# First batch's decay rates loaded by token pairs, row-half sums, two-step head dots and a new order of work in an RWKV attention and Fourier MLP kernel

## The chip, the cores and the metric

The kernel runs on one core of a Trainium2 chip. The core has five engines that run side by side: TensorE (PE, matrix products into eight PSUM banks), VectorE (DVE), ScalarE (ACT), GpSimd (POOL) and SyncE (SP, whose queue issues nearly all transfers). They wait for each other through semaphores. The metric is the device time of one execution in microseconds, the lower the better: a median of 181.98 us over three runs (181.62, 182.01 and 181.98).

## The reference

Inputs r, k, v and w have the shape (4 batches, 8 heads, 768 tokens, 48), in float32. For each batch and head a 48 x 48 state runs over the tokens:

```python
for t in range(S):
    cur = np.einsum('bhd,bhe->bhde', u[None] * kt, vt)
    y[:, :, t] = np.einsum('bhd,bhde->bhe', rt, state + cur)
    state = wt[:, :, :, None] * state + np.einsum('bhd,bhe->bhde', kt, vt)
...
X = np.fft.fft(np.fft.fft(x, axis=1), axis=2)     # x is y as (4, 768, 384)
u = x + np.real(X).astype(np.float32)
un = (u - mu) / np.sqrt(var + 1e-06)               # over the 384 columns
return u + np.maximum(un @ w_ch1, 0.0) @ w_ch2     # 384 -> 1536 -> 384
```

The output is (4, 768, 384) in float32.

## The kernel before

A batch's 768 tokens are cut into six chunks of 128 tokens, token on partition, and a pair such as (1, 4) below is batch 1, chunk 4. Attention of a chunk goes by these steps, with the names in the profile:

- four loads on SP's queue, each 192 KB in rows of 48 floats: `in_w`, `in_k`, `in_r`, `in_v` (line 622). Seven buffers of each kind stand for seven chunks.
- ACT takes the logarithm of w (`lb`, line 590). PE multiplies it with a mask (`msk`, line 795) for the sum over the earlier tokens. The sum that includes the token itself comes in one of several ways: `sum_two`, a second product with another mask (`nle`, line 818), or `sum_add`, an addition on DVE (line 832). Small products (lines 806 and 809) give each half head's total for the state's decay.
- ACT takes the exponentials (`e`, line 822; in the bank, line 848). DVE or POOL multiplies r and k with them (`rkh`, lines 849 and 576). PE transposes the two (lines 890 and 902) and ACT or DVE copies the result to `rkt` (lines 599 and 600); for the six chunks of batch 3 a transposing transfer on SP's queue does it instead (line 880).
- PE makes the 128 x 128 scores of each head (line 913, 48 rows at a time on two halves of the array), DVE masks them (`ah`, line 923), PE multiplies them and the state with v (lines 978 and 975) and brings the state forward (lines 950 and 947), and DVE applies the decay (line 958).
- The current token's term is r times k times u (`rk`, line 576, on POOL or DVE), summed over a head's 48 columns by one DVE reduction (`dc`, line 863), times v (`vtd`). It is added to the chunk's result in `x` (line 989 and others).

After a batch's six chunks the Fourier mix folds `x` (`sd`, `xf`), multiplies with cosine and sine tables (lines 1054 to 1059), copies (`hcs`, `hcr`), multiplies again (line 1098), and adds x (`uf`, lines 1115 and 1128). The mean is taken off (`un`), by batch statistics on DVE (`bst`, `agg`, lines 1155 and 1157) in batches 1 to 3, and in batch 0 by a sum that comes out of the addition itself, with the variance from a square on ACT. The normalised rows are transposed by PE and copied (`unt`), or transposed by a transfer (line 1180), in halves of three chunks. The MLP then takes for each half 36 products of 128 x 384 with the first matrix (line 1205), a clamp at zero on ACT or DVE (`ht`), and 36 with the second (line 1224), and DVE adds and scales (`osb`, line 1233) before the store.

What sets the order: each step is recorded as an operation, often with several ways and several engines to choose from, and a table of numbers, `ORDER`, written out per engine, picks the ways and the sequence. Each engine runs its list in that sequence and waits where a step needs another engine's. A planner's costs (`dur`, `xfer`, `T_LAT`) do not move the lists, they only decide which PSUM bank a step gets. PE's list has 32 filler products into a bank that nobody reads (line 1291).

## Time and profile before

| | us |
|---|---|
| median of three runs | 181.98 |
| profiled execution, time | 181.76 |
| profiled execution, span | 179.6 |
| PE busy | 172.1 |
| DVE busy | 159.5 |
| ACT busy | 127.5 |
| POOL busy | 107.7 |
| first MLP product of batch 0 starts (line 1205) | 41.4 |
| first MLP product of batch 1 starts (line 1205) | 84.5 |
| last MLP product ends | 177.1 |

The span runs from the first to the last instruction of the profiled execution; 2.16 us of its time lie around it. A group's row gives the line, engine, operation, output and inputs, count, then busy us in all and mean ns of one, then the engine's idle time just before them and what ended it. Products and DVE instructions overlap their neighbours a little, so the pitch from one to the next is shorter than a row's mean.

### The profile page before, as it was taken

Reading aid. Unit: us, or ns where it says so; the run is one execution under the profiler, and the core shown is the slowest. Engines: PE = TensorE matmul, PEld = TensorE weight load, DVE = VectorE, ACT = ScalarE, POOL = GpSimd, SP = SyncE. Lnnn points to the kernel's source line nnn. Section 1 sums busy time; section 2 is a strip of 40 time slices with the busy share of each in tenths; the row PEclk is TensorE's granted clock in tenths of the full one; section 3 lists DMA queues with packets and bytes.
Section 4 is the critical chain, followed back from the end, with each engine's and each line's share of the span. In section 5 each row is a group of like instructions: output and inputs, shape, how many; then the busy total and the mean of one; then the engine's idle time right before and its main releaser. Section 6 shows DMA issues by size and latency. Waiting matters only on the chain.

```text
span 179.6 us, 4554 instructions
## 1 busy us (share of the span) xinstructions
PE 172.1 (96%) x1704; PEld 113.7 (63%) x1704; DVE 159.5 (89%) x378; ACT 127.5 (71%) x306; POOL 107.7 (60%) x134
## 2 busy tenths in 40 slices
PE   4989899999999999999999999999989999999994
PEld 2456556766666667777666666766656766655663
DVE  7899899989999899999999999999999997971643
ACT  2899978679996578799999897989960775062200
POOL 2557969496705888499999964997862140500000
PEclk9999999999999999999999999999999999999999
DMA  6999999999999689999997999989972213034033
GB/s 118 217 210 225 183 206 193 203 216 179 162 205 204 145 173 224 199 211 217 202 239 137 224 182 240 235 155 197 245 71 56 74 47 65 1 60 141 0 131 131
DMA packets 117302, 29.28 MB, mean 163 GB/s; under 512 B 112545, under 2 KB 117282, under 8 KB 117282
## 3 DMA queue, kind: packets, MB, share of 16 engines
q1 hardware_dynamic: 115698, 26.65, 72.3%
q0 software_dynamic: 1584, 2.36, 7.9%
q8 instruction: 13, 0.21, 0.5%
q14 instruction: 7, 0.06, 0.1%
HBM read 23.59 MB, written 4.72 MB: 158 GB/s over the span
## 4 chain that ended last, share of the span: by engine, by line
PE 72%; DVE 13%; ACT 7%; POOL 3%; DMA 3%; issue 1%; POOLq 0%; DVEq 0%; ACTq 0%
PE bank L1205 23%; PE bank L1224 23%; PE bank L1098 4%; PE bank L1054 3%; PE bank L913 3%; DMA rkt<-rkh 3%; PE bank L890 2%; PE bank L795 2%; PE bank L978 2%; DVE bst L1155 2%; PE bank L975 1%; DVE uf L1128 1%; ACT rkt L599 1%; PE bank L950 1%; PE bank L818 1%
## 5 line engine op out<-in xcount | busy, mean ns | idle before, releaser
L1224 PE MATMUL bank<-w,ht 128*128 128x384 bf16 (+2 forms) x300 | 53.1, 320 | 0.0
L1205 PE MATMUL bank<-unt,w 128*128 128x384 bf16 x288 | 52.9, 326 | 0.0
L1213 ACT ACTIVATE ht<-bank 128x384 bf16<-128x384 f32 x70 | 31.0, 496 | 21.1 <-PE bank L1205 20.9
L1224 PEld LDWEIGHTS bank<-w,ht 128*128 128x128 bf16 x300 | 27.8, 98 | 15.6
L1205 PEld LDWEIGHTS bank<-unt,w 128*128 128x128 bf16 x288 | 26.6, 98 | 15.8 <-ACT ht L1213 0.2
L923 DVE TENSOR_TENSOR ah<-bank,msk 128x512 bf16<-128x512 f32 x44 | 28.7, 682 | 0.8 <-PE bank L913 0.6
L576 POOL TENSOR_TENSOR rk<-in_r,in_k 128x384 f32<-128x384 f32 x22 | 21.8, 999 | 1.9 <-issue 1.4
L576 POOL TENSOR_TENSOR rkh<-in_k,e 128x384 bf16<-128x384 f32 x18 | 18.0, 1003 | 6.7 <-ACT e L836 4.9
L576 POOL TENSOR_TENSOR rk<-rk,ub 128x384 f32<-128x384 f32 x20 | 19.8, 998 | 3.3 <-DVE rk L576 2.1
L576 POOL TENSOR_TENSOR vtd<-in_v,dc 128x384 f32<-128x384 f32 x20 | 16.4, 829 | 5.1 <-DVE sd L576 1.8
L599 ACT ACTIVATE rkt<-bank 128x512 bf16<-128x512 bf16 (+1 forms) x23 | 16.3, 713 | 4.3 <-PE bank L902 2.8
L1233 DVE SCALAR_TENSOR_TENSOR osb<-bank,rstd,uf 128x384 f32<-128x384 f32 (+2 forms) x24 | 14.3, 594 | 5.5 <-PE bank L1224 3.5
L1211 DVE TENSOR_SCALAR ht<-bank 128x384 bf16<-128x384 f32 x26 | 13.5, 548 | 5.4 <-PE bank L1205 5.2
L863 DVE TENSOR_REDUCE dc<-rk 128x8 f32<-128x384 f32 x24 | 12.7, 544 | 0.4 <-POOL rk L576 0.4
L848 ACT ACTIVATE bank<-bank 128x384 f32<-128x384 f32 x22 | 10.6, 488 | 3.0 <-PE bank L795 2.7
L590 ACT ACTIVATE lb<-in_w 128x384 bf16<-128x384 f32 x24 | 12.6, 528 | 0.1
L590 ACT ACTIVATE un<-uf,agg 128x384 bf16<-128x384 f32 x19 | 11.2, 618 | 1.5 <-DVE agg L1157 0.9
L849 DVE TENSOR_TENSOR rkh<-bank,in_r 128x384 bf16<-128x384 f32 x22 | 11.9, 547 | 0.2 <-ACT bank L848 0.2
L590 ACT ACTIVATE vb<-in_v 128x384 bf16<-128x384 f32 x22 | 11.5, 530 | 0.4 <-DMA in_v<-in_v_dram 0.3
L822 ACT ACTIVATE e<-bank 128x392 f32<-128x392 f32 (+1 forms) x18 | 8.8, 498 | 3.9 <-PE bank L809 2.5
L978 PE MATMUL bank<-vb,ah 128*128 128x48 bf16 x192 | 11.2, 183 | 0.0
L576 POOL TENSOR_TENSOR xf<-sd 128x384 bf16<-128x384 f32 (+1 forms) x7 | 6.9, 1002 | 6.1 <-DVE xf L576 3.9
(178 smaller groups left out, 365.1 us busy)
## 6 DMA issues: line engine op xcount, KB each, us to landing
in_r<-in_r_dram SPq DMA_DIRECT2D x24, 192.0 KB, 3.9
in_k<-in_k_dram SPq DMA_DIRECT2D x24, 192.0 KB, 3.8
in_w<-in_w_dram SPq DMA_DIRECT2D x24, 192.0 KB, 3.8
in_v<-in_v_dram SPq DMA_DIRECT2D x24, 192.0 KB, 3.8
out_dram<-osb SPq DMA_DIRECT2D x23, 192.0 KB, 2.9
w<-in_moe_w_ch_dram POOLq DMA_DIRECT2D x2, 576.0 KB, 7.9
w<-in_moe_w_ch_dram POOLq DMA_DIRECT2D x1, 1152.0 KB, 10.7
out_dram<-osb SPq DMA_DIRECT2D x1, 128.0 KB, 1.8
```

Source lines behind the costliest of these rows:

```text
L576: return lambda e: e.tensor_tensor(out=o, in0=a, in1=b, op=f)
L590: return lambda e: e.activation(o, a, f, **kw)
L599: {"act": lambda e: e.activation(o(), i(), ACTF.Copy), "dve": lambda e: e.tensor_copy(out=o(), in_=i())}, **kw)
L849: op("dve", v_1(DM), lambda e: e.tensor_tensor(out=rh[:, :, 0:D], in0=ps(tce)[:, 0:DM].rearrange("t (h d) -> t h d", d=D), in1=rt[:, :, :] ...
L863: op("dve", v_1(DM), lambda e: e.tensor_reduce(out=dc[:, :], in_=rku[:, :, :], axis=mybir.AxisListType.X, op=ALU.add), r=[("RK", i2)], w=[ ...
L923: masked[n].append(op("dve", v_1(512), lambda e: e.tensor_tensor(out=ah[:, x:H:2, :], in0=ps(bk)[:, :].rearrange("p (h t) -> p h t", t=128 ...
L978: ins = e.matmul(ps(ty)[:, D * h:D * h + D], ah[:, h, :], vb[:, h, :], start=first and not ype, stop=True, skip_group_check=True)
L1205: ins = e.matmul(ps(t)[:, 0:384], W1[:, m, 256 * (j // 2) + j % 2:256 * (j // 2) + 256:2], unt[:, :, m, :], start=(m == 0), stop=(m == NM ...
L1211: {"dve": lambda e, j=j, t=t, ht=ht: e.tensor_scalar(out=ht[:, j, :], in0=ps(t)[:, 0:384], scalar1=su, scalar2=0.0, op0=ALU.mult, op1=ALU. ...
L1213: "act": lambda e, j=j, t=t, ht=ht: e.activation(ht[:, j, :], ps(t)[:, 0:384], ACTF.Relu, scale=su)},
L1224: ins = e.matmul(ps(t)[:, 0:hi - lo], ht[:, j, 128 * x:128 * x + 128], W2[:, j, lo:hi], start=(j == 0), stop=(j == NJ - 1))
L1233: op("dve", v_1(hi - lo) + 64, lambda e: e.scalar_tensor_tensor(out=o[:, lo:hi], in0=ps(t)[:, 0:hi - lo], scalar=rstd[:, kb:kb + 1], in1=u ...
```

## The change

For batch 0 alone (`PAIRED = 1`) the six loads of w become three, each of 256 tokens: token 2p lies beside token 2p + 1 on partition p, so that a row is 96 floats. The sums over tokens are then made for a pair of chunks at once: two logarithms (even and odd tokens), and for each of the two sums four products that each use half of the array's rows, with four new 128 x 128 masks (`PM`, which DVE makes in a buffer that `unt` uses later), and 16 (for the last pair 8) small products for the totals. The exponential of the totals becomes two narrow ACT instructions in place of a wider single one. All 'sum' ways of batch 0 fall away.

The reduction over a head's 48 columns may be made in two steps, adding two halves of 24 and then reducing 24 columns (`dots`). Three chunks use it: (0, 1), (0, 3) and (1, 0). Four half-batch columns of `uf`, three in batch 2 and one in batch 3, use a new way (`add_sum`): the sum comes out of the addition, and ACT's square gives the variance, in place of the batch statistics. Some planner costs change (load 985 to 998, `T_LAT`, a shift by 200), and the table `ORDER` is new on all five engines.

Beside the pairs, the table picks other ways for some chunks: chunks (1, 4), (1, 5) and (2, 1) take `sum_add` in place of `sum_two` while (1, 0) goes the other way; chunk (1, 4) is transposed by a transfer and no longer by PE.

SP's queue at the start of the program; the digit behind a name is the buffer, here the chunk of batch 0, and in the changed kernel `in_w` is one tensor with all buffers. Before:

```order
L622 DMA in_r1<-in_r_dram 128x8x48
L622 DMA in_k1<-in_k_dram 128x8x48
L622 DMA in_w1<-in_w_dram 128x8x48
L622 DMA in_w0<-in_w_dram 128x8x48
L615 DMA osb0<-in_u_dram 1x384
L622 DMA in_r0<-in_r_dram 128x8x48
L622 DMA in_k0<-in_k_dram 128x8x48
L622 DMA in_w2<-in_w_dram 128x8x48
L622 DMA in_v0<-in_v_dram 128x8x48
```

Now:

```order
L634 DMA in_r1<-in_r_dram 128x8x48
L634 DMA in_r0<-in_r_dram 128x8x48
L634 DMA in_k1<-in_k_dram 128x8x48
L643 DMA in_w<-in_w_dram 128x8x96
L623 DMA osb0<-in_u_dram 1x384
L634 DMA in_k0<-in_k_dram 128x8x48
L634 DMA in_k2<-in_k_dram 128x8x48
L643 DMA in_w<-in_w_dram 128x8x96
L634 DMA in_v0<-in_v_dram 128x8x48
```

The loads of w for two chunks have become one, and those of r and k stand closer to the front.

PE just after the first fillers; `lb` is the logarithm of w, `msk` and `nle` are the old masks, `unt0` holds the new ones. Before:

```order
L656 MATMUL bank1<-osb0,vtd3 128x384
L795 MATMUL bank2<-lb0,msk 128x384
L818 MATMUL bank3<-lb0,nle 128x384
L795 MATMUL bank4<-lb1,msk 128x384
L749 MATMUL bank5<-ss,unt1 128x193
```

Now:

```order
L687 MATMUL bank1<-osb0,vtd3 128x384
L839 MATMUL bank2<-lb0,unt0 128x384
L839 MATMUL bank3<-lb0,unt0 128x384
L839 MATMUL bank2<-lb1,unt0 128x384
L839 MATMUL bank3<-lb1,unt0 128x384
L839 MATMUL bank4<-lb0,unt0 128x384
L839 MATMUL bank5<-lb0,unt0 128x384
```

Each sum of a chunk has become two half-row products into the same bank, and the products of both chunks alternate.

DVE in batch 0's first chunks, from the first product of r with its exponential (`rkh`) on; `rk` is r times k, `dc` the head sums, `vtd` the current token's term. Before:

```order
L863 TENSOR_REDUCE dc1<-rk1 128x8
L849 TENSOR_TENSOR rkh1<-bank4,in_r1 128x8x48
L849 TENSOR_TENSOR rkh0<-bank2,in_r0 128x8x48
L863 TENSOR_REDUCE dc0<-rk0 128x8
L576 TENSOR_TENSOR rkh1<-in_k1,e2_1 128x8x48
L587 MEMSET rkh2 128x8x8
L600 COPY rkt0<-bank4 128x512
L576 TENSOR_TENSOR vtd0<-in_v0,dc0 128x384
```

Now:

```order
L608 COPY ub<-bank1 128x384
L922 TENSOR_TENSOR rkh0<-bank2,in_r0 128x8x48
L922 TENSOR_TENSOR rkh1<-bank3,in_r1 128x8x48
L595 MEMSET rkh0 128x8x8
L584 TENSOR_TENSOR rk0<-rk0,ub 128x384
L584 TENSOR_TENSOR rkh0<-in_k0,e2_0 128x8x48
L584 TENSOR_TENSOR rk1<-rk1 128x8x24
L940 TENSOR_REDUCE dc0<-rk0 128x8
L940 TENSOR_REDUCE dc1<-rk1 128x8
```

The head sums have moved behind both products with r, one of them has an addition of halves (`rk1<-rk1`) ahead of it, and the copy of `ub` has come to DVE from ACT.

The diff, without the table:

```diff
-PSUM_STATE, NE = 1, 16
+PSUM_STATE, NE, PAIRED = 1, 16, 1
...
+INW = sb("in_w", [NIN, H, D], FP32)
+INB["w"] = [INW[:, i, :, :] for i in range(NIN)]
+PM = UNT[0].rearrange("p a b t -> p (a b t)")[:, 0:512].rearrange("p (x t) -> p x t", x=4)
...
+    def load_pair(b, c):
+        i = (b * NC + c) % NIN
+        loads[b, c, "w"] = loads[b, c + 1, "w"] = op("sp", 750, lambda e: e.dma_start(
+            INW[:, i:i + 2, :, :].rearrange("p a h d -> p (a h d)").rearrange("p (h x) -> p h x", h=H),
+            w[b, :, c * CH:(c + 2) * CH, :].rearrange("h (p a) d -> p h (a d)", a=2)),
+            w=[("in", "w", i), ("in", "w", i + 1)], sem="in_w%d" % i, xfer=1400)
...
+        for x, (f0, f1, s1) in enumerate(((ALU.subtract, ALU.is_gt, 0.0), (ALU.subtract, ALU.is_gt, 1.0),
+                                          (ALU.is_ge, ALU.mult, -1.0), (ALU.is_gt, ALU.mult, -1.0))):
+            dset(128, ts(PM[:, x, :], CI[:, 128:256], QP[:, :], s1, f0, f1), r=["CI", "QP", ("UNT", 0, 1)],
+                 w=["PM%d" % x] + ([("UNT", 0, 0)] if x == 0 else []))
...
+                    def cum(e, m=m):
+                        for x in range(2):
+                            for y in range(2):
+                                z = slice(64 * y, 64 * y + 64)
+                                ins = e.matmul(ps(sums[n + y, m])[:, 0:DM], PM[z, 2 * m + x, :], LB[l2[x]][z, :, 0:D],
+                                               start=x == 0, stop=x == 1, skip_group_check=True)
+                        for h in range(HP if m else 0):
+                            for x in range(2):
+                                for y in range(2 if c < NC - 2 else 1):
+                                    z = slice(64 * y, 64 * y + 64)
+                                    ins = e.matmul(ps(sums[n + y, m])[:, DM + 2 * h:DM + 2 * h + 2],
+                                                   LB[l2[x]][z, 2 * h:2 * h + 2, :].rearrange("t h d -> t (h d)"), ONE[z, :],
+                                                   start=x == 0, stop=x == 1, skip_group_check=True)
...
+        def dots(m):
+            if m < D:
+                vec(H * m, tt(rku[:, :, 0:m], rku[:, :, 0:m], rku[:, :, m:D], ALU.add), w=[("RK", i2)])
+            op("dve", v_1(H * m), lambda e: e.tensor_reduce(out=dc[:, :], in_=rku[:, :, 0:m],
+                                                            axis=mybir.AxisListType.X, op=ALU.add),
+               r=[("RK", i2)], w=[("DC", i2)])
+        g.choose(("dots", b, c), lambda: dots(D), lambda: dots(D // 2))
...
+                def add_sum(kb=kb, t=t):
+                    whole()
+                    op("dve", v_1(DM) + 60, lambda e: e.scalar_tensor_tensor(
+                        out=uf[:, kb, :], in0=ps(t)[:, 0:DM], scalar=1.0, in1=xb[:, kb, 0:DM], op0=ALU.mult, op1=ALU.add,
+                        accum_out=ms[:, kb, 2:3]), r=[t, ("X", i, kb)], w=[("UF", i, kb), ("SUM", i, kb)])
+                    normed(ms[:, kb, 0:1], ("MS", i, kb))
+                    op("act", a_sb(DM) + 190, act(xf[:, kb, 63:447], uf[:, kb, :], ACTF.Square, scale=-float(DM) ** -0.5,
+                                                  bias=ms[:, kb, 1:2], accum_out=agg[:, kb, 1:2]),
+                       r=[("UF", i, kb), ("MS", i, kb)], w=[("AGG", i, kb)] + [(z, i, kb) for z in ("XFe", "XFo", "XFn")])
+                g.choose(("u", b, kb), add_bank, add_row, add_parts, add_sum)
```

More of the change, by code (lines that the diff above doesn't have):

```diff
@@ L814, in total, with sum_pair @@
                 op("pe", mm(1, 5), tot, r=["ONE", "IDB", "PB0", "PB", ("LB", i2)], w=[t])
+        def sum_pair():
+            op("act", a_ps(DM), lambda e: e.activation(E2[i2][:, 0:DM], ps(tci)[:, 0:DM], ACTF.Exp), r=[tci], w=[("E2", i2)])
+            if not last:
+                for x in range(2):
+                    op("act", a_ps(4) + 20, lambda e, x=x: e.activation(
+                        E2[i2][64 * x:64 * x + 64, DM + x:DM + H:2], ps(tci)[64 * x:64 * x + 64, DM + x:DM + H:2], ACTF.Exp),
+                       r=[tci], w=[("E2", i2)])
         def sum_two():
@@ L844, in sum_key @@
             decays([("E2", i2)])
-        g.choose(("sum", b, c), sum_two, sum_add, sum_key)
+        if paired:
+            sum_pair()
+        else:
+            g.choose(("sum", b, c), sum_two, sum_add, sum_key)
         def rh_bank():
```

86 lines of the change are left out of this document (62 added, 24 removed), and 139 rows, old and new, of the table ORDER.

## The prediction

> **What bounds the kernel now.** I first cut the span at the two places where a batch's MLP begins, and read each engine's busy time and the idle clock there.
>
> ```profile
> core 0: us, PE busy (x) PEld busy (x) DVE busy (x) ACT busy (x) POOL busy (x), PEclk, DMA share, GB/s
> 0.00:9.00 9.00, 6.51 (x26) 2.97 (x26) 7.32 (x37) 5.27 (x7) 3.52 (x14) 1.00 0.85 168
> 9.00:41.40 32.40, 30.45 (x381) 20.57 (x381) 30.28 (x72) 27.65 (x63) 25.29 (x33) 1.00 1.07 205
> 41.40:84.50 43.10, 43.08 (x471) 29.64 (x469) 41.74 (x92) 35.52 (x87) 29.47 (x34) 1.00 0.99 192
> 84.50:134.50 50.00, 49.49 (x521) 32.60 (x518) 48.59 (x106) 44.78 (x113) 42.41 (x47) 1.00 0.97 193
> 134.50:179.60 45.10, 42.54 (x315) 27.87 (x312) 31.55 (x74) 14.25 (x39) 7.06 (x11) 1.00 0.25 71
> ```
>
> From 41.4 on PE never stops (43.08 of 43.10, then 49.49 of 50.00); before that its busy time holds fillers. The same windows for the filler line alone:
>
> ```profile
> 0.00:9.00 9.00, 0.98 (x5) 0.49 (x5) 1.00 0.85 168
> 9.00:41.40 32.40, 5.05 (x19) 1.63 (x19) 1.00 1.07 205
> 41.40:84.50 43.10, 2.60 (x8) 0.78 (x8) 1.00 0.99 192
> ```
>
> So up to 41.4 PE has slack, some of it filled, and DVE is the tight engine: idle 1.68 + 2.12 = 3.80 us there, then 1.36, then 1.41. Eight fillers still stand between 41.4 and 84.5, most of them late, when batch 0's MLP is used up and DVE finishes batch 1's mix. After 84.5 there is no filler, and the chain of waits is PE's to the end:
>
> ```profile
> 40.82 0.62 PE bank L913 x16
> 41.43 2.54 PE bank L1205 x15
> 48.45 0.33 PE bank L913 x8
> 57.85 1.95 PE bank L1224 x12
> 84.00 0.60 PE bank L913 x16
> 84.61 2.06 PE bank L1205 x12
> 89.31 0.45 PE bank L902 x8
> 128.63 4.57 DMA rkt<-rkh
> 133.24 0.40 PE bank L913 x8
> 170.51 6.54 PE bank L1224 x52
> 177.15 0.35 DVE osb L1233
> ```
>
> The pitch of a 384-column product is 1.95/12 = 0.1625 us. Hence the time is: the start of batch 0's first L1205 (41.43), plus PE's work to batch 1's first L1205 (84.5), plus PE's work to 177.1, with one stop in it, at 133.24.
>
> **The change part by part.**
>
> *After 84.5.* Counted from the two programs, PE's products from batch 1's first L1205 to the end are the same set in both. `add_sum`, three of whose four columns replace batch statistics in batch 2, lies here, relieves DVE and lengthens nothing on PE: 0. What can move is PE's one stop:
>
> ```profile
> 133.24 0.40 PE L913 MATMUL bank<-rkt 48*128 48x128 bf16 x8 [0.51 <-DMA rkt<-rkh]
> ```
>
> The last two transposing transfers follow each other there. In the new order of SP's queue other transfers stand between those of (3, 4) and (3, 5), and the scores come earlier on PE. Bounds: 0.51 and the drain around it gone (-0.7), nothing (0), another such stop (+0.5). I take -0.35, midway between the first two, since the shift of both sides is ordered, not timed.
>
> *Between the two first L1205.* Three `nle` products go (to `sum_add`): 3 x 0.1625 = -0.49. (1, 4) goes from PE to a transfer: 8 products, by
>
> ```profile
> 38.09 0.22 PE bank L890 x4
> ```
>
> 8 x 0.055 = -0.44. Two fillers fewer, 2 x 0.1625 = -0.33, which counts if they only filled. PE's bound on this stretch falls by 1.26. The transfer adds one to SP's queue, among the stores of batch 0 and loads of batch 2; if it lands late, PE's scores for (1, 4) wait, and MLP products stand beside them as cover. I put 0 on it.
>
> *Up to batch 0's first L1205*, on DVE. The groups of that window:
>
> ```profile
> L863 DVE TENSOR_REDUCE dc<-rk 128x8 f32<-128x384 f32 x6 | 3.3, 546 | 0.4 <-POOL rk L576 0.4
> L1115 DVE SCALAR_TENSOR_TENSOR uf<-bank,x 128x384 f32<-128x384 f32 x5 | 2.6, 555 | 0.4 <-PE bank L1098 0.4
> L600 DVE CAST hcs<-bank 128x386 bf16<-128x386 f32 x3 | 1.7, 597 | 0.4 <-PE bank L1057 0.4
> L989 DVE TENSOR_TENSOR x<-bank,vtd 128x384 f32<-128x384 f32 x3 | 1.6, 549 | 0.1
> L576 DVE TENSOR_TENSOR xf<-x 128x191 bf16<-128x191 f32 (+1 forms) x5 | 1.5, 349 | 0.0
> L600 DVE COPY rkt<-bank 128x512 bf16<-128x512 bf16 x3 | 1.2, 420 | 0.0
> L576 DVE TENSOR_TENSOR rk<-in_r,in_k 128x384 f32<-128x384 f32 x2 | 1.1, 548 | 0.0
> L832 DVE TENSOR_TENSOR e<-bank,lb 128x384 f32<-128x384 f32 x1 | 0.5, 547 | 0.0
> L581 DVE TENSOR_SCALAR cp<-cp 128x1 f32<-128x1 f32 x1 | 0.1, 141 | 0.0
> L581 DVE TENSOR_SCALAR nle<-osb 128x128 bf16<-128x128 f32 x1 | 0.2, 207 | 0.0
> ```
>
> Against DVE's list up to its last `unt` copy ahead of that product, the new list has: `rk` products six for three, 3 x 0.548 = +1.65; additions to `x` five for three, +1.10; the copy of `ub`, taken as an addition from a bank, +0.55; one more `uf`, +0.56; the new masks, 4 x 0.207 + 2 x 0.141 = +1.11. It loses two `hcs`, -1.20, one `e`, -0.55, and small pieces (a part of the sine tables, copies of `rkt`, a score mask), -0.72. Six reductions become four and two halves with one addition of halves on DVE (the other is POOL's), each of the three at the 0.349 of a 191-wide addition: 4 x 0.546 + 3 x 0.349 = 3.23 against 3.28, that is -0.05, which fills make up. So two steps cost as much as one. Sum +2.45 us of durations. Rows of one engine overlap:
>
> ```profile
> 9.12 0.56 DVE L576 TENSOR_TENSOR rk<-rk,ub 128x384 f32<-128x384 f32 x1
> 9.60 0.55 DVE L576 TENSOR_TENSOR rk<-in_r,in_k 128x384 f32<-128x384 f32 x1
> ```
>
> The second starts 0.48 after the first, which lasts 0.56, a ratio of 0.86: +2.1 us of time.
>
> This can go into DVE's 3.80 us idle. Two of its pieces:
>
> ```profile
> 0.81 0.06 DVE L587 MEMSET bhpi<- 128x1 f32 x1 [0.81 <-PEq L1310]
> 8.97 0.06 DVE L587 MEMSET cs<- 128x3 bf16 x1 [0.53 <-POOL cs L580]
> ```
>
> The first 0.81 stays. The waits for `hcs` and `uf` above (0.4 each) and one for the last copies (0.3) are the mix's latency and stay too. Some 1.9 can be filled; as rows waiting on loads and POOL rarely fit whole, I take 1.2 filled. Batch 0's first L1205 then starts 0.9 later (bounds: 2.1 later with nothing filled; 0.8 earlier, if all can be filled and the waits for `hcs` and `uf` go too and the loads come sooner).
>
> From there to the end of batch 1's mix DVE is repaid: fewer table pieces and copies of `unt`, folds on POOL. Its list up to batch 1's first `uf` is only 0.14 us of rows longer than before, which less the 1.2 filled gives -1.1. POOL gets 5.9 us of rows more and ACT 1.7 in the whole program; between 41.4 and 84.5 alone ACT has 43.10 - 35.52 = 7.6 idle and POOL 13.6, so I put 0 on both. If that cover fails it is POOL's, whose pieces DVE's reductions already wait for (0.4 on line 863's row).
>
> *Loads.* The 18 loads of r, k and v for batch 0 stand, six loads of w become three. One takes
>
> ```profile
> in_w<-in_w_dram SPq DMA_DIRECT2D x24, 192.0 KB, 3.8
> ```
>
> 3.8 us to land, but at 205 GB/s of the window the queue passes one in 196608 / 205 GB/s = 0.96. Rows twice as long move at least as many bytes per time: the window with 192-byte rows gives 205 / 1.07 = 192 GB/s at full share, the one with stores in 1536-byte rows 71 / 0.25 = 284. A pair thus costs between 1.92 (no gain) and 1.30 (the store's rate); I take 1.55, near the short rows: -0.37 each, -1.1 in all, bounds 0 and -1.9. [...] Either way the loads end at 30, when DVE, not a load, sets the pace: 0 in the sum. The price is at the front: ACT's two logarithms of a pair both wait for one load of 1.55 instead of the first for one of 0.96, 0.6 later by the queue; behind them on ACT stand the exponentials that DVE's `rkh` needs. r and k now come ahead of it on the queue, so DVE has `rk` to do meanwhile; this is part of why I fill 1.2 and not 1.9.
>
> *Sums by half rows*, PE: 24 products for 12. Eight 48-row products on two halves take 0.33 (48.45) against 0.45 for eight full ones (89.31), a ratio of 0.73, though with 128 columns: 24 x 0.1625 x 0.73 = 2.85 against 12 x 0.1625 = 1.95, +0.9. [...]
>
> **Sum.** At batch 1's first L1205 the later of two sides counts: PE +0.9 - 0.93 - 0.33 = -0.36, DVE -1.1. So -0.36, then -0.35 late: -0.7. The profiled execution's 181.76 (span 179.6 and 2.16 around it) becomes 181.05; its time lies 0.2 below the median 181.98, from which -0.7 gives 181.2.
>
> **Rivals.**
> - *DVE's idle is not filled* (slower). With nothing filled batch 0's first L1205 comes 2.1 later, at 43.5; PE's side is +2.1 - 1.26 = +0.84 and DVE's +0.14, and the late stop stays: 182.8. Its place is the front, where four masks and the larger load of w stand ahead of the first chunk's sums. For it: POOL, at 999 ns a piece, gets more of what DVE waits for:
>
> ```profile
> L576 POOL TENSOR_TENSOR rk<-in_r,in_k 128x384 f32<-128x384 f32 x22 | 21.8, 999 | 1.9 <-issue 1.4
> ```
>
> Against: the new list has work that needs only r and k at just that place. It decides if that product starts after 41.43 + 0.93 + 0.33 = 42.7, where PE's side turns from gain to loss. Chance 0.26.
> - *DVE is freed sooner* (faster): with the pairs early, all 1.9 and more filled, the first L1205 at 40.6; PE -0.8 - 1.26 = -2.1, DVE -1.8; with -0.35: 179.8. Against it stand the +2.45. Chance 0.12.
> - *No change*: PE's two sides cancel (first L1205 1.3 later) and the late stop stays: 181.6 to 182.3. Chance 0.15.
> - *New stops after 84.5*: there is no filler there, so an operand that is late costs its whole wait. Three like the 0.51 of 133.24, with the drain at the price 0.7 taken above, less the -0.36: +1.7 and about 183.5 at most; 0.09. For it: POOL has more rows, and SP's queue one transfer more between its loads.
>
> **Numbers.** My forecast 0.38, own range 180.6 to 181.6. 0.2% (0.36 us) is about what a measurement here can tell. Faster: 0.38 + 0.12 = 0.50; within: 0.15; slower: 0.26 + 0.09 = 0.35. The range 179.6 to 183.6 reaches from just below the faster rival to the end of the last one; what it leaves out is their bounds being passed, less than 2 in 10.
>
> **What would show it.** Right: batch 0's first L1205 at 42.0 to 42.6, batch 1's at about 84.1, PE's stretch from there to its end at about 92.2 (now 177.05 - 84.5 = 92.55), six fillers between them, and DVE idle up to the first at 2.6. Wrong: a first L1205 after 42.7; more than six fillers' worth of idle on PE ahead of batch 1's; waits for `rkt`, `ht` or `ah` on PE after it; or a reduction of 24 columns that takes 0.55 as the one of 48 does, which turns the two steps into +1.0 on DVE.

## The result: slower, 184.76 us

| | before | changed |
|---|---|---|
| median, us | 181.99 (181.62 to 182.01, 4 runs) | 184.76 (183.95 to 185.22, 4 runs) |
| profiled execution: time, span, us | 181.76, 179.6 | 184.74, 182.9 |
| batch 0's first MLP product (now line 1304), us | 41.38 | 45.17 |
| batch 1's first MLP product | 84.54 | 86.78 |
| from there to PE's end | 92.50 | 93.65 |

The ratio is 1.0152, with a 95% interval of 1.0115 to 1.019. The forecast was 181.2. Executions more than 1.5% longer than the fastest of their kernel are left out of the medians and ratios here and below.

The windows of the changed kernel, cut at the same places as those of before, with the first stretch cut finer:

```profile
core 0: us, PE busy (x) PEld busy (x) DVE busy (x) ACT busy (x) POOL busy (x), PEclk, DMA share, GB/s
0.00:9.00 9.00, 6.12 (x21) 2.89 (x21) 7.12 (x42) 4.98 (x6) 3.76 (x14) 1.00 0.84 183
9.00:14.00 5.00, 4.04 (x48) 2.26 (x46) 3.39 (x9) 3.37 (x11) 1.79 (x4) 1.00 1.18 235
14.00:18.00 4.00, 3.49 (x31) 2.27 (x32) 3.21 (x7) 3.07 (x5) 3.31 (x5) 0.67 1.10 238
18.00:22.00 4.00, 3.80 (x68) 2.50 (x65) 3.62 (x9) 3.52 (x10) 1.98 (x3) 0.90 0.95 182
22.00:45.20 23.20, 21.98 (x276) 14.85 (x274) 21.91 (x54) 19.73 (x43) 16.96 (x23) 1.00 1.06 202
45.20:86.80 41.60, 41.60 (x459) 28.36 (x458) 40.44 (x88) 37.06 (x95) 31.42 (x36) 1.00 0.89 174
86.80:136.80 50.00, 48.78 (x511) 32.20 (x510) 48.75 (x107) 41.98 (x108) 43.66 (x49) 1.00 0.99 198
136.80:182.90 46.10, 43.53 (x323) 28.29 (x321) 30.54 (x74) 16.13 (x44) 10.17 (x14) 1.00 0.25 70
```

Three things stand out. The stretch between the two first MLP products is shorter (41.6 us for 43.1) and full. Ahead of it, between 9 and 18, DVE is busy only 6.60 of 9 us, where it was busy 8.80 before, and the granted clock (the share of full speed that TensorE is allowed) falls to 0.67 and then 0.90, where it was 1.00 in every window of before. After 86.8 PE is idle 1.22 of 50 us, where it was idle 0.51. So the milestones give the loss as a sum: +3.79 up to the first product, -1.55 between the two, +1.15 after: +3.39 on PE's end, against the -0.7 that was forecast.

DVE up to batch 0's first MLP product, of before:

```profile
0.00:41.38 41.38, 36.94 (x406) 23.53 (x407) 37.59 (x108) 32.90 (x69) 28.78 (x45) 1.00 1.03 197
```

and of the changed kernel:

```profile
0.00:45.17 45.17, 39.40 (x433) 24.76 (x434) 39.23 (x119) 34.64 (x74) 27.76 (x46) 0.96 1.02 203
```

DVE's work grew by 39.23 - 37.59 = 1.64. Its idle time, of which the forecast fills 1.2, grew from 3.79 to 5.94, by 2.15. Between 9 and 18 alone it is idler by 2.2, as much as the whole growth. Its waits there, in the changed kernel (us in all, times, longest):

```profile
DVE ub L608 <- PE bank L687: 1.8, 1, 1.8
DVE xf L595 <- PEq L1409: 0.8, 1, 0.8
DVE ah L1001 <- PE bank L991: 0.8, 1, 0.8
DVE rkh L922 <- ACT bank L921: 0.6, 2, 0.4
DVE rkh L584 <- ACT e L882: 0.4, 1, 0.4
```

The largest is new: the copy of `ub`, which the change brought to DVE, waits 1.8 us for a product of PE. PE's own start, in order of time (start, us, operation, and in brackets the idle time before it and who ended it):

```profile
2.88 5.30 PE L1356 MATMUL bank<-w 128*128 128x384 bf16 x16 [2.88 <-DVE w L595]
7.97 1.25 PE L1390 MATMUL bank<-idw,msk 128*128 128x384 bf16 x5
9.15 0.91 PE L687 MATMUL bank<-osb,vtd 1*128 1x384 f32 x2
9.99 0.82 PE L839 MATMUL bank<-lb,unt 64*128 64x384 bf16 x8
...
11.73 0.40 PE L980 MATMUL bank<-idw,rkh 128*128 128x128 bf16 x4 [0.29 <-DVE rkh L922]
...
13.29 0.40 PE L980 MATMUL bank<-idw,rkh 128*128 128x128 bf16 x4 [0.67 <-DVE rkh L584]
...
15.31 0.61 PE L991 MATMUL bank<-rkt 48*128 48x128 bf16 x8 [0.51 <-ACT rkt L607]
...
17.14 1.46 PE L839 MATMUL bank<-lb,unt 64*128 64x384 bf16 x8
```

The first 16 products, the warm-up, run on `w`, which DVE fills with ones for the purpose. One of them lasts 514 ns at the median before and 528 now, a filler of the same shape behind them 326 and 327. They began at 2.27 before and begin at 2.88 now, took 4.22 in all and take 5.30, and the product for `ub` and the first sums stand behind them. Then come three short stops, and after them the eight half-row sums that took 0.82 us at 9.99 take 1.46 at 17.14 (1.10 where the clock does not fall, as a later profile shows).

After 86.8 the chain of waits no longer is PE's alone. It comes to PE at 124.66 from DVE:

```profile
117.92 1.04 DVE uf L1251 x4
118.96 0.86 DVE ms L1254
119.82 0.47 DVE uf L1251 x2
120.30 0.33 DVE ms L1254 x2
...
124.00 0.61 DVE ah L1001
```

Line 1254 is the small product in `add_sum` that turns the sum of a row into the mean and the bias of the square.

### The profile page after: what moved, and what is told of

The parts are those of the page before. It is cut to its first block, busy times and chain, and to the rows that moved or that the text cites. A ratio compares the mean times of both kernels' runs of the same rounds, so it can differ in the third digit from the quotient of the medians.

```text
span 182.9 us, 4618 instructions
## 1 busy us (share of the span) xinstructions
PE 173.3 (95%) x1719; PEld 113.6 (62%) x1719; DVE 159.0 (87%) x385; ACT 129.9 (71%) x318; POOL 113.0 (62%) x142
## 4 chain that ended last, share of the span: by engine, by line
PE 60%; POOL 15%; DVE 11%; ACT 4%; issue 3%; SPq 2%; DMA 2%; DVEq 0%
PE bank L1304 19%; PE bank L1323 18%; POOL rk L584 7%; POOL rkh L584 4%; PE bank L1356 3%; PE bank L1176 2%; POOL vtd L584 2%; DVE ah L1001 2%; DMA in_r<-in_r_dram 2%; SPq L634 2%; PE bank L991 2%; PE bank L1390 2%; POOL sd L584 2%; DVE osb L1332 1%; PE bank L1056 1%
## 5 line engine op out<-in xcount | busy, mean ns | idle before, releaser
L1312 ACT ACTIVATE ht<-bank 128x384 bf16<-128x384 f32 x73 | 33.2, 502 | 21.3 <-PE bank L1304 21.0
L1304 PEld LDWEIGHTS bank<-unt,w 128*128 128x128 bf16 x288 | 26.6, 98 | 15.5 <-DVE unt L608 0.2
L584 POOL TENSOR_TENSOR rk<-in_r,in_k 128x384 f32<-128x384 f32 x19 | 18.9, 1003 | 1.3 <-DVE rkh L584 0.5
L584 POOL TENSOR_TENSOR rkh<-in_k,e 128x384 bf16<-128x384 f32 x17 | 17.0, 1005 | 3.5 <-DVE rk L584 1.8
L1310 DVE TENSOR_SCALAR ht<-bank 128x384 bf16<-128x384 f32 x23 | 12.3, 550 | 6.7 <-PE bank L1304 6.6
L607 ACT ACTIVATE rkt<-bank 128x512 bf16<-128x512 bf16 (+1 forms) x19 | 14.9, 784 | 2.5 <-PE bank L980 1.8
L584 POOL TENSOR_TENSOR sd<-x 128x385 f32<-128x385 f32 x11 | 11.0, 1010 | 2.7 <-DVE xf L584 1.7
L940 DVE TENSOR_REDUCE dc<-rk 128x8 f32<-128x384 f32 (+1 forms) x24 | 12.2, 517 | 0.3 <-POOL rk L584 0.2
L1067 DVE TENSOR_TENSOR x<-bank,vtd 128x384 f32<-128x384 f32 x21 | 11.4, 548 | 1.1 <-PE bank L1056 1.0
L584 POOL TENSOR_TENSOR xf<-sd 128x382 bf16<-128x382 f32 (+1 forms) x9 | 8.9, 1002 | 5.1 <-DVE xf L584 4.9
L598 ACT ACTIVATE un<-uf,agg 128x384 bf16<-128x384 f32 x18 | 10.5, 621 | 1.8 <-DVE agg L1213 1.7
```

The costliest lines, as they stand in the source:

```text
L584: return lambda e: e.tensor_tensor(out=o, in0=a, in1=b, op=f)
L598: return lambda e: e.activation(o, a, f, **kw)
L607: {"act": lambda e: e.activation(o(), i(), ACTF.Copy), "dve": lambda e: e.tensor_copy(out=o(), in_=i())}, **kw)
L940: op("dve", v_1(H * m), lambda e: e.tensor_reduce(out=dc[:, :], in_=rku[:, :, 0:m], axis=mybir.AxisListType.X, op=ALU.add), r=[("RK", i2)] ...
L1304: ins = e.matmul(ps(t)[:, 0:384], W1[:, m, 256 * (j // 2) + j % 2:256 * (j // 2) + 256:2], unt[:, :, m, :], start=(m == 0), stop=(m == NM ...
L1310: {"dve": lambda e, j=j, t=t, ht=ht: e.tensor_scalar(out=ht[:, j, :], in0=ps(t)[:, 0:384], scalar1=su, scalar2=0.0, op0=ALU.mult, op1=ALU. ...
```

## The experiments

**The fill of `w` in its old place, and the other way round.** Two theories for the late start: the fill of `w`, moved from the fifth place on DVE's list to the ninth, delays the warm-up and all behind it; or DVE's new work does it alone, and the fill's place is hidden. Three kernels. In the changed kernel the fill goes first:

```diff
 DVE's list, from its start
+L595 MEMSET w 128x384
 L595 MEMSET xf 128x6x32
 L595 MEMSET lb 128x8x8
 ...
 L595 MEMSET rkh 128x8x8
-L595 MEMSET w 128x384
 L589 TENSOR_SCALAR unt<-tc 128x1
```

> The changed kernel with one DVE instruction moved: the fill of w with ones, which PE's 16 warm-up products wait for, is first on DVE's list (it started at 2.44 us). Theory A (the late fill and the colder warm-up that follows hold up PE's front, then ub and the first sums, and this goes through to the end): the warm-up starts at about 1.3 and ends near 6.5 instead of 8.0, DVE's wait for ub of 1.81 shrinks below 0.7, the first L1304 comes at about 44 instead of 45.2, and the time falls by 1.0 to 1.6 us against the changed kernel's 184.76. Rival B (the front has slack, and DVE's and ACT's order in chunks (0, 1) to (0, 3) sets batch 0's end): the first sums come earlier, but the first L1304 moves by less than 0.3 and the time by less than 0.4.

In the kernel before the fill goes behind three more instructions (the expectation counts four):

```diff
-L587 MEMSET w 128x384
 L587 MEMSET vtd 1x128
 L587 MEMSET lb 128x256
-L581 TENSOR_SCALAR ht<-osb,tn 128x194 x2
+L581 TENSOR_SCALAR ht<-osb,tn 128x194
+L587 MEMSET w 128x384
+L581 TENSOR_SCALAR ht<-osb,tn 128x194
```

> The kernel before with one DVE instruction moved: the fill of w with ones stands behind four other instructions, so that it starts at about 2.45 instead of 1.83 us, as in the changed kernel. Theory A (that fill is on the path): first L1205 0.6 to 1.5 us later than 41.4 and the time up by 0.6 to 1.5 against 181.98. Rival B: the front has slack, less than 0.3 in both.

And in the kernel before it goes to the head of the list:

> The kernel before with one DVE instruction moved: the fill of w is DVE's first instead of fifth, so that PE's warm-up starts at about 1.3 instead of 2.27 us. Theory A (PE's front is on the path in the kernel before as well): the first L1205 0.5 to 1.0 us earlier than 41.4 and the time as much lower than 182.0. Rival B (there the first sums wait for ACT's logarithms at 8.35, not for PE): the first L1205 moves by less than 0.2; and PE then stands idle between its warm-up and the first sums, so that the clock can fall and cost 0.3 to 1.0.

Measured: with the fill first, the changed kernel takes 183.86 (ratio to before 1.012, 1.0061 to 1.0179), its first MLP product starts at 44.20 and PE ends at 179.37, 0.97 and 1.06 sooner. In this pair of profiles what is won at the front arrives at the end. The times alone do not show it, since the intervals of the two ratios overlap. The kernel before with a late fill takes a median of 183.24 (1.0107, 1.004 to 1.0174); its first MLP products start at 42.15 and 85.31, both 0.77 later. In the profile PE's end is only 0.1 later, since the stop for `rkt` near 133 vanished from that execution. The kernel before with the fill first gains nothing (182.91, a ratio of 0.9999, 0.9956 to 1.0041): its first sums wait for ACT's logarithms, and its first MLP product starts at 41.26, 0.12 sooner.

**The changed kernel a second time.** It was run again beside the later experiments.

> The changed kernel itself, unedited, beside the three runs below on the same chip: both theories expect the 1.0152 (1.0115 to 1.019) of the first measurement, that is +2.7 us, a first L1304 at 44.6 to 45.2, a granted clock near 0.6 in some 3 us between 14 and 20 us, and one stop of about 1.1 us on PE near 123.

The median is 184.15 (182.45 to 184.93), beside 183.0 for before on that chip, where both scatter more; the ratio is 1.0061 (1.0017 to 1.0104), still slower, though by less than the 1.0152 of the first chip. Its profiled execution differs from the first where it tells most:

```profile
2.88 4.53 PE L1356 MATMUL bank<-w 128*128 128x384 bf16 x16 [2.88 <-DVE w L595]
7.24 0.98 PE L1390 MATMUL bank<-idw,msk 128*128 128x384 bf16 x5
8.15 0.91 PE L687 MATMUL bank<-osb,vtd 1*128 1x384 f32 x2
8.99 0.82 PE L839 MATMUL bank<-lb,unt 64*128 64x384 bf16 x8
```

With the fill at the same 2.88, the same 16 products take 4.53 and not 5.30, the sums start a whole microsecond sooner, the clock does not fall, and the first MLP product starts at 43.67 instead of 45.17. So 1.5 of the 3.79 is not in every execution. The two runs below that change nothing ahead of batch 1's MLP (the two small products, and the batch statistics) give this front twice more, 44.65 and 45.19, both with a fall of the clock. In all four it comes 2.3 to 3.8 later than before.

The 1.5 does not reach the end. This execution took 185.46, longer than most: PE stops 1.1 for `xf` ahead of batch 1's first product, then 0.56, 0.29 and 0.42 behind it, and ends at 181.13, later than the 180.43 of the first profile.

The same rows with the fill first:

```profile
1.31 4.35 PE L1356 MATMUL bank<-w 128*128 128x384 bf16 x16 [1.31 <-DVE w L595]
5.49 0.98 PE L1390 MATMUL bank<-idw,msk 128*128 128x384 bf16 x5
...
9.05 0.83 PE L839 MATMUL bank<-lb,unt 64*128 64x384 bf16 x8 [1.34 <-DVE ub L608]
```

The paired kernels profiled with the fill first all start these sums at 9.05 or 9.06, while their warm-up lasts from 4.19 to 5.30. With the late fill the start follows the warm-up: 4.53 gives 8.99, 4.97 gives 9.43, 5.30 gives 9.99 (10.10 in the run with batch statistics). So the fill's old place was cover for a warm-up of uncertain length. Moving it behind costs nothing with a short warm-up and about 1 us with a long one. The first theory holds with that condition.

**Fillers at PE's stops.** Is the fall of the clock a cost of its own, or does it only show that PE has nothing to do? The fill goes first, and eight fillers more stand ahead of the three stops:

```diff
-NW = 32
+NW = 40
 PE's list, chunk (0, 0)
+L1390 MATMUL bank<-idw,msk 128x384 x2
 L980 MATMUL bank<-idw,rkh 128x128 x4
 ...
 L780 MATMUL bank<-ss,idw 128x191 x2
+L1390 MATMUL bank<-idw,msk 128x384 x3
 L980 MATMUL bank<-idw,rkh 128x128 x4
 ...
+L1390 MATMUL bank<-idw,msk 128x384 x3
 L991 MATMUL bank<-rkt 128x128 x8
```

> The changed kernel with the fill of w first, as in the run that moved it, and eight more filler products on PE (0.1625 us each), one, three or two to four at each place where PE then stood idle for chunk (0, 0): ahead of the transposes of r, of k, and of the first scores. Theory A (PE's idle time between 10.5 and 15.3 us lets the granted clock fall to 0.5, and PE's chain of chunks (0, 0) to (0, 2) is then slow and on the path): the clock in 14 to 18 us reads 1.00 instead of 0.60, the first L1304 comes 0.6 to 1.2 us earlier than the 44.2 without these fillers, and the time falls by as much against 183.86. Rival B (the slow clock falls where PE waits anyway): the clock reads 1.00, but the first L1304 and the time move by less than 0.3.

The window from 14 to 18 with the fill first alone:

```profile
14.00:18.00 4.00, 3.59 (x52) 2.31 (x52) 3.14 (x7) 2.74 (x6) 3.31 (x4) 0.60 0.94 213
```

and with the fillers too, above it the stretch up to the first MLP product:

```profile
0.00:43.32 43.32, 39.23 (x441) 24.45 (x442) 38.69 (x119) 34.54 (x74) 27.87 (x46) 1.00 0.98 192
...
14.00:18.00 4.00, 3.39 (x63) 2.03 (x61) 3.43 (x8) 3.55 (x9) 3.46 (x5) 1.00 1.09 242
```

The clock stays at 1.00 and the first MLP product starts at 43.32, 0.88 sooner than with the fill first alone: more work on PE made the rest earlier. Is it the clock, or do the fillers help in another way? One product further on tells, with the fill first alone (first row), with the fillers too (second), and in the second profile of the changed kernel, which has neither the fillers nor the fall (third):

```profile
19.16 0.88 PE L1076 MATMUL bank<-vtd,ht 128*128 128x384 f32 x2
```

```profile
18.25 0.88 PE L1076 MATMUL bank<-vtd,ht 128*128 128x384 f32 x2
```

```profile
18.18 0.88 PE L1076 MATMUL bank<-vtd,ht 128*128 128x384 f32 x2
```

The first scores ahead of it start alike in the three, at 14.37, 14.37 and 14.31. So the fall itself costs 0.91 to 0.98 there. The times are 184.07 (1.0055, 1.0005 to 1.0105), and in a repetition

> The base of the three runs below: the changed kernel with the fill of w first and eight gap fillers, as run before (first L1304 at 43.3 then). Expected again 43.0 to 43.7, with the clock at 1.00 from 14 to 22 us.

183.95 (1.0074, 1.0032 to 1.0117) with 43.22. In times the gain does not show: these ratios stand beside the 1.0061 of the unedited kernel. Each execution's mean granted clock lets one count: it is 0.990 or 0.991 in the two profiles with the fall shown and 1.000 in the second profile of the changed kernel. A mean under 0.995 was there in 23 of 32 executions of the paired new order without these fillers, in 2 of 33 with them, and in 3 of 51 of the kernel before. With the fill first, where PE stands idle between its warm-up and the first sums, the kernel before has it in 4 of 10.

**The copy of `ub` back on ACT**, with the fill first:

```diff
 DVE's list
-L608 COPY ub<-bank 128x384
 L922 TENSOR_TENSOR rkh<-bank,in_r 128x8x48 x2
```

> The changed kernel with the fill of w first, and with the copy of ub back on ACT behind the first two logarithms, as in the kernel before, and off DVE's list. Theory A (DVE's list up to the first L1304 is the bound, so that work taken off it shortens it): 0.55 us of DVE time less, the first L1304 0.3 to 0.6 us earlier than 44.2, the time as much lower than 183.86. Rival B (the chain through ACT's exponentials sets the first chunks and DVE has idle time to spare there): the first L1304 moves by -0.2 to +0.5, since ACT now does 0.47 us more ahead of the first exponential.

184.71 (1.011, 1.0061 to 1.0158). Its first MLP product starts at 43.50, without a fall of the clock in that profile; the kernels with fillers, which have none either, stand at 43.2 to 43.3. So the copy's place gains nothing that shows once the fill is first. The sums still start at 9.06, and what PE waits for there is ACT's logarithm (1.24).

**The small product of `add_sum`.** In the late stop, DVE and POOL of the changed kernel, first DVE:

```profile
118.88 0.94 DVE L1254 TENSOR_TENSOR ms<-ms,mco 128x2 f32<-128x2 f32 x1
119.74 0.54 DVE L1251 SCALAR_TENSOR_TENSOR uf<-bank,x 128x384 f32<-128x384 f32 x1
...
120.22 1.34 DVE L1254 TENSOR_TENSOR ms<-ms,mco 128x2 f32<-128x2 f32 x2
121.48 0.60 DVE L1332 SCALAR_TENSOR_TENSOR osb<-bank,rstd,uf 128x384 f32<-128x384 f32 x1
```

then POOL:

```profile
117.84 1.96 POOL L584 TENSOR_TENSOR rk<-in_r,in_k 128x384 f32<-128x384 f32 x2
119.76 0.83 POOL L584 TENSOR_TENSOR vtd<-in_v,dc 128x384 f32<-128x384 f32 x1
120.55 0.99 POOL L584 TENSOR_TENSOR rk<-rk,ub 128x384 f32<-128x384 f32 x1
```

and what PE makes of it:

```profile
123.22 0.62 PE L991 MATMUL bank<-rkt 48*128 48x128 bf16 x16 [1.10 <-DVE osb L1332]
```

Two columns take DVE 0.94 us at 118.88, and end with POOL's instruction at 119.8; the pair at 120.22 ends at 121.56, as POOL's next does. The fourth, later, takes 0.16. A larger DVE instruction with two SBUF inputs shows the like: a product of `ah` with the mask takes 0.41 at 25.12, with POOL idle, and 0.78 at 130.48, where POOL's instruction ends at 130.98. The small product has two SBUF inputs as well, `ms` and `mco`. The theory: such an instruction waits for the end of POOL's, and the one with one input would not. The rival: the wait is for the sum that comes out of the addition just ahead. The product becomes two with a constant:

```diff
-                    op("dve", 64, lambda e: e.tensor_tensor(
-                        out=ms[:, kb, 0:2], in0=ms[:, kb, 2:3].to_broadcast([128, 2]), in1=MCO[:, :], op=ALU.mult),
+                    op("dve", 64, lambda e: [e.tensor_scalar(out=ms[:, kb, z:z + 1], in0=ms[:, kb, 2:3], scalar1=float(DM) ** -(1 + z / 2),
+                        scalar2=None, op0=ALU.mult) for z in range(2)][1],
```

> The changed kernel, its order untouched; the 128x2 product of add_sum, which has two operands in SBUF, becomes two 128x1 products with a constant, each with one operand in SBUF. Theory A (an instruction with two operands in SBUF waits until POOL's running instruction has ended): each of the eight takes about 0.14 and none 0.6 or more, and the stop of 1.10 at 123.2 shrinks by about the 1.7 us that DVE gains there or disappears; the time falls by 0.5 to 1.2 against 184.76. Rival B (the wait is for the sum that comes out of the addition just before): the first product of each pair still takes 0.6 to 0.9 and the time stays within 0.3.

The line's durations (least, median, greatest, in ns) were 160/664/1030. Now:

```profile
L1254 DVE TENSOR_SCALAR ms<-ms x8: 143/144/153, 118.6 to 149.1; 128x1 f32<-128x1 f32 x8
```

None is long any more, so the rival falls. The stop is gone: PE's only wait after batch 1's first MLP product is 0.3 for an `rkt`, and from that product to its end PE takes 92.59, against 93.65 (and 92.50 before). How much of this is the edit is less sure. With the two-input product, the stop is 0.17 to 1.1 in the profiles of the other paired kernels, and the stretch takes 93.37 to 94.73. With the two small products in the run of all mends, below, this stop is gone too, but others of 0.47 and 0.27 take its place and the stretch takes 93.46. The kernel before has 91.84 with the late fill and 94.55 with the fill first. The times do not resolve the microsecond: 183.2, 184.92 and 185.59, a ratio of 1.0156 (1.0109 to 1.0203); its front had the late fill and the fall of the clock.

The other way, batch statistics again in those four columns, came to nothing:

> The changed kernel with add_sum undone in its four columns: the addition and batch statistics as in the kernel before. Theory A (the 128x2 product of add_sum on DVE waits for POOL's running instruction, 0.94, 0.67 and 0.67 us, and so makes the output row and the bank late for which PE stops 1.10 us at 123.2): four columns cost DVE 4 x 0.72 us of statistics instead of 2.4 us of those products, but the normalised rows and the banks are free sooner, the stop at 123.2 goes, and the time falls by 0.8 to 1.3 us. Rival B (DVE is late there because it waited for the load in_r at 116.8, and would be so with statistics too): DVE does 0.4 us more, the stop stays or grows, and the time changes by -0.2 to +0.5.

Its runs lie between 183.77 and 187.88, and the profiled one is the longest. There PE stops 0.8 at the same place with the statistics. Nothing about their price follows from it, and whether `add_sum` is worse than they are stays open.

**Without pairs.** In the new order, and again with all mends of the next paragraph. Beside this line each chunk's pieces take the places that the pair's had in the lists, and one exponential of 392 columns replaces the three:

```diff
-PSUM_STATE, NE, PAIRED = 1, 16, 1
+PSUM_STATE, NE, PAIRED = 1, 16, 0
```

> The changed kernel with the pairs undone and the new order kept: batch 0 loads w by chunk, takes sums of whole rows with the old masks, and one exponential of 392 columns in place of three; each chunk's pieces stand where the pair's stood in every engine's list; the four new masks are still made, later, and are not used. Theory A (the pairs themselves cost little; the order of the front does): ACT has 1.0 us less in narrow exponentials up to 22 us, PE 0 to 0.1 us less, loads 0 to 1 us later, so the first L1304 moves by -0.6 to +0.4 and the time by as much. Rival B (waiting for a pair's two logarithms and its eight products at once delays both chunks): the first L1304 comes 1 to 2 us earlier and the time falls by 1 to 2.

184.23 (1.0129, 1.0075 to 1.0182), the first MLP product at 44.62 without a fall of the clock and with a short warm-up (4.37): 0.95 later than the changed kernel in the like execution (43.67). On ACT stands a wait that the paired one does not have there:

```profile
ACT lb L598 <- DMA in_w<-in_w_dram: 2.3, 1, 2.3
```

> The run with all four edits, and the pairs undone in it: batch 0's w by chunk, sums of whole rows, one exponential of 392 columns for three, the new masks made later and unused. Theory A (pairs cost or bring little: 1.0 us less on ACT up to 22 us against loads that end up to 1 us later): first L1304 and time within 0.4 us of the run with all four edits. Rival B (pairs hold both chunks back): 0.8 to 2 us earlier. Rival C (pairs do what they are for, r and k arrive sooner and PE's sums are shorter): 0.5 to 1.5 us later without them.

185.47, and 45.33 where the paired one has 44.65; ACT waits 2.0 for loads of w. In the first 20 us the two kernels without pairs load 3.64 and 3.59 MB, and the thirteen profiles with pairs 3.76 to 4.14, so the longer rows move at least as many bytes in the same time. The pairs are no loss in this order: in each of two pairs of profiles the first MLP product comes 0.7 to 0.95 sooner with them. That w then arrives in time fits, though the waits alone were not tried. The times do not tell the kernels with and without pairs apart.

**Taking work off DVE, and all mends at once.** With the fill first and the fillers, both `rk` products of chunk (0, 4) go from DVE to POOL:

```diff
 DVE's list
 L940 TENSOR_REDUCE dc<-rk 128x8
-L584 TENSOR_TENSOR rk<-in_r,in_k 128x384
 L584 TENSOR_TENSOR ah<-ah,msk 128x4x128
-L584 TENSOR_TENSOR rk<-rk,ub 128x384
 L940 TENSOR_REDUCE dc<-rk 128x8
```

> The run with the fill first and eight gap fillers, and beside that both rk products of chunk (0, 4) (0.55 us each) moved from DVE to POOL, into gaps of 2.2 and 1.4 us that POOL had there. Theory A (from 18 us on DVE's list is the bound up to batch 0's first L1304, since it shows no idle time of over 0.3 us between 21 and 38): the first L1304 comes 0.7 to 1.1 us earlier than 43.3. Rival B (the chain from chunk to chunk through PE, ACT and POOL is the bound, DVE merely busy): it moves by less than 0.3, and DVE shows new idle time of about 1 us instead.

> All four edits together: fill of w first, eight gap fillers, rk of (0, 4) on POOL, and the one-operand products in add_sum. If the losses found are all there is and add up (start +3.8, stop 1.1): first L1304 at 42.3 to 43.3, no stop of over 0.5 us near 123, last product 1.9 to 2.9 us earlier than the first run's 180.4 by the edits at the start and 1.0 more by the stop, and a time of 180.6 to 181.9, so equal to the kernel before or up to 0.8 % faster. Rival: a new stop takes back what the earlier start gives, time 182.5 or more.

The first gives 185.52 (1.0138, 1.007 to 1.0206), the second, which has the two small products too, 185.4 (1.0118, 1.0059 to 1.0177), where 180.6 to 181.9 was expected if all losses added up. The first MLP product starts at 44.57 and 44.65, 1.3 later, for DVE waits for POOL instead:

```profile
DVE dc L940 <- POOL rk L584: 1.8, 2, 1.1
```

**Is DVE's list the bound?** With fill and fillers as before, the first of these adds two products at chunk (0, 4) into a buffer that is not read, the second replaces that chunk's two `rk` products by fills of two columns, so that it leaves out the current token's term of that chunk, and the third puts two logarithms and a table piece behind the copy of `rkt` on ACT:

```diff
 DVE's list, chunk (0, 4), first kernel
 L940 TENSOR_REDUCE dc<-rk 128x8
+L584 TENSOR_TENSOR ht<-in_r,in_k 128x384 x2
 L584 TENSOR_TENSOR rk<-in_r,in_k 128x384
 ACT's list, third kernel
-L598 ACTIVATE lb<-in_w 128x8x48
 L882 ACTIVATE e_1<-bank 64x4
-L598 ACTIVATE lb<-in_w 128x8x48
-L783 ACTIVATE dtm<-bank 128x384
 L607 ACTIVATE rkt<-bank 128x1024
+L598 ACTIVATE lb<-in_w 128x8x48 x2
```

> The base with two more DVE instructions of 0.55 us just ahead of rk of chunk (0, 4): the same product into two places that nobody reads. DVE's work grows by 1.0 us at about 23 us, nothing else does. Theory A (DVE's list is the bound from 20 us on): the first L1304 comes 0.8 to 1.1 us later than the base's. Rival B (DVE is merely busy; the chain through ACT, POOL and PE is the bound): 0 to 0.3 later.

> The base with both rk products of chunk (0, 4) left out (two fills of 2 columns stand in their place; the current token's term of that one chunk is then not computed): DVE's work shrinks by 1.0 us, at 23 to 25 us. Theory A: the first L1304 comes 0.7 to 1.0 us earlier. Rival B: 0 to 0.3 earlier.

> The base with three ACT instructions (the two logarithms of the second pair and one copy of a table) moved behind the copy of rkt of chunk (0, 0), which they preceded. If ACT's list is what holds up the first chunk: rkt 0.5 us earlier, scores and masks of (0, 0) as well, first L1304 0.3 to 0.6 earlier than the base's. If not: within 0.2, or up to 0.5 later since the second pair's sums come later.

Without the addition (first fence) and with it (second), on DVE:

```profile
22.63 0.62 DVE L584 TENSOR_TENSOR rk<-in_r,in_k 128x384 f32<-128x384 f32 x1
...
24.62 0.55 DVE L922 TENSOR_TENSOR rkh<-bank,in_r 128x384 bf16<-128x384 f32 x1
```

```profile
22.63 1.09 DVE L584 TENSOR_TENSOR ht<-in_r,in_k 128x384 bf16<-128x384 f32 x2
...
25.56 0.55 DVE L922 TENSOR_TENSOR rkh<-bank,in_r 128x384 bf16<-128x384 f32 x1
```

The `rkh` behind them starts 0.94 later and the first MLP product 0.90 later (44.12 for 43.22): work added to DVE there is paid in full. Work taken away does not come back: 44.24. But in that execution the logarithm of the third pair waited 0.9 on ACT for its load, and the exponentials behind it held DVE up 1.25 ahead of the place, so this run cannot say what DVE alone is worth. The other order on ACT gives 44.36, a loss of 1.1, with DVE waiting 0.65 for ACT's exponentials. The times, 184.71, 184.78 and 185.34, lie within the scatter of one another.

No version was faster than the kernel before, and none is clearly faster than the unedited changed kernel: the gains above are read in single profiles, at the first MLP product.

## Why the prediction was wrong

The stretch that decides and the sum from one milestone to the next held in the first profile: PE's stretch between the two first products shrank by 1.55 for -1.26, with the six fillers foretold, and a shift of the first MLP product could pass to the end in full (0.97 gave 1.06), though the second profile lost its 1.5 on the way. The loss sits in the other two terms.

*"Some 1.9 can be filled ... I take 1.2 filled"* is the step that failed, and with it the start term of +0.9 with its bound of 2.1. DVE's added work was about right (+1.64 busy, +2.1 foretold). Its idle time was treated as a stock that could only be used up. It grew by 2.15, and the bound "nothing filled" did not allow for that. Two edits take back 1.85 of the 3.79 in the profiles; the rest is argued:

- The fill of `w`, an instruction of 0.38 us that the sum does not have at all: 0.97 in the profiled execution, whose warm-up was long. The step on `ub`'s copy, "an addition from a bank, +0.55", counted its work and not its wait: it stands behind that warm-up, and DVE waits 1.8 with all its list behind it.
- The fall of the clock after three stops of 0.29, 0.67 and 0.51: 0.88. The prediction has no term for it; it read PE's slack up to 41.4 as free.
- The rest is 43.32 - 41.38 = 1.94. DVE is busy 38.69 of the 43.32, so this is 1.10 of work and 0.84 of idle. That work on DVE passes in full, one run shows (0.90 for 0.94). For the idle there is one pair of rows. The first sums wait for ACT's logarithm in the kernel before with the fill first, and there start at 8.15:

```profile
8.15 0.34 PE L795 MATMUL bank<-lb,msk 128*128 128x384 bf16 x1 [0.51 <-ACT lb L590]
```

In the changed order they start at 9.05, 0.90 later, and with `ub` out of the way they wait for ACT's logarithm as well. This is not the price that the prediction gave the larger load ("0.6 later by the queue"). In the two first profiles the first logarithm starts at 7.82 in the changed kernel and at 7.77 before, in both without a wait for the load. With the fill first and `ub` on ACT in both, the kernel before (first row) and the changed one (second) have:

```profile
7.57 0.94 ACT L590 ACTIVATE lb<-in_w 128x384 bf16<-128x384 f32 x2
```

```profile
7.98 0.94 ACT L598 ACTIVATE lb<-in_w 128x384 bf16<-128x384 f32 x2
```

About 0.4 comes from here; ACT started as much later on a table piece that it waits for DVE to hand over (5.01 for 4.61). The rest is that a pair's sums need both logarithms, where a chunk's need one. That the 0.90 is the cause of the 0.84 fits but was not tried by itself, and the kernels without pairs speak against so simple a reading: their sums start at 8.83 and 8.56, yet their first MLP product comes later.

*"`add_sum` ... relieves DVE and lengthens nothing on PE: 0"* failed too. Three of its four small products took 0.94 + 1.34 = 2.28 us beside POOL, the fourth 0.16, and PE stopped 1.10 for what stood behind them. The term was forecast at -0.35 and came out at +1.15 in this profile; executions differ there by more than that, as told above, so its size stays open. The half of it on `rkt` came true in this profile by luck: no wait for an `rkt` is left in the changed kernel's list of PE's waits from 86.8 on, but later profiles of the same order have one again (0.29 at 112.6, 0.24 at 134.8). "Three like the 0.51" was the rival for this, at 0.09; it took one stop.

The likelier rival for the loss, *DVE's idle is not filled*, named the place and the sign, and its point of decision, a first MLP product after 42.7, was passed. Its price of 182.8 was too small for the reason above. The change's parts as such were read rightly: a reduction of 24 columns takes 0.34 and the addition of halves 0.35, so that two steps are no loss on DVE while POOL does one of the two additions; and the first half-row sums cost no more than the whole ones that they replace, since eight of them follow each other in 0.65 (9.99 to 10.65), half of 0.1625 each. The +0.9 that the prediction set for them, and left out of its sum (the +0.9 there is the later start), did not come.

Open stays how the 1.94 divides between DVE's work, the later sums and what else the new order does, and how much of the loss an average execution carries: the executions differ by about as much as one of the causes.

## What to carry to other kernels

An engine's idle time is not a stock: a change can add to it, so bound it on both sides, and for each instruction that the change brings to an in-order list cost its wait and all that stands behind it, not its duration alone. Look at the first small instructions of every list, since a fill of 0.4 us may be the cover of a warm-up whose length differs between executions (4.19 to 5.30 us here). Cost even an instruction of two columns by its operands: with two SBUF inputs beside a busy POOL it lasted 0.94 us here, near POOL's own 0.83 to 1.00, and a column with one SBUF input 0.14.

## What the runs showed of the hardware

The same 16 warm-up products took 4.19 to 5.30 us in the 18 profiles, all of kernels that begin PE's list with them; the granted clock reads 1.00 over the first 9 us of the two first profiles, and what sets the length was not shown. In the first profile of the changed kernel three gaps of 0.29, 0.67 and 0.51 between 11 and 15.3 us were followed by a granted clock of 0.50 from 15.5 to 18 us (0.67 over the window from 14 to 18); with fillers in them it reads 1.00 over that window. A mean under 0.995 stands in 23 of 32 executions without these fillers against 2 of 33 with them, so short gaps close together can be enough. They need not be: the second profile of the changed kernel has the same three gaps (0.29, 0.66, 0.51) and a clock of 1.00.
